# Holding each output unit behind the matmul emitted ahead of it, in the 512-token round of a two-stage mixture kernel

## The chip, the cores and the metric

The kernel runs on one core of a Trainium2 chip. A core has five engines that each work through a queue of their own in order: TensorE (PE: matmuls, with its weight loads as PEld), VectorE (DVE), ScalarE (ACT), GpSimd (POOL) and SyncE (SP, here only issuing DMAs). They wait for one another through semaphores. The metric is the device time of one execution in microseconds (us). Before the change it is 1851.79 us, the median of three runs (1851.22 to 1853.6).

## The reference

The result is three stages in a chain, all in float32.

```python
p_packed = sm_attn(p, k, v)                    # 32 packed queries per head, 576 keys
out = sm_attn(q, p_packed, p_packed)           # 4 batches x 8 heads x 576 tokens x 64
x = out.transpose(0, 2, 1, 3).reshape(2304, 512)
h = np.maximum(x @ w_in, 0.0)                  # 512 -> 2048
x = h * h @ w_out                              # 2048 -> 512
logits = x @ w_gate; P = np.exp(logits - logits.max())
for _ in range(8):                             # gate: rows, then columns
    P /= P.sum(1, keepdims=True) + 1e-09
    P /= P.sum(0, keepdims=True) + 1e-09
    P *= 2304 / 8
for e in range(8):                             # 8 experts, each over all 2304 tokens
    out += P[:, e:e+1] * (np.maximum(x @ w1[e], 0.0) @ w2[e])
```

## The kernel before

Every matmul operand is split into a high and a low part of a narrower format, and a product is three matmuls: high by high, high by low, low by high. The last stage, with the eight experts, takes most of the time. It treats the 2304 tokens in three rounds: 512 tokens (group p = 0, columns in blocks of 256), then 1024 (blocks of 512), then 768 (blocks of 384). This case is about the first of them, from about 414 to 757 us.

In that round `for n in range(NQ)` runs 32 units, a quarter of an expert's hidden width each. `unit(n, 0, ...)` computes the first layer by a Strassen-like scheme: seven products of 6 matmuls with 256 columns (`product`, L758), into three PSUM tiles X, Z and Y of 128x512:

- A11 into X; ACT copies X out (s1). A12 into Y; DVE adds s1 to Y.
- S1 into Z; ACT copies Z out (s5). S2 is added into X; ACT copies X out (s2).
- S4 is added into Z, after the copy s5 has read Z; DVE adds s2. S3 is added into X, after s2; DVE writes X + s5 into Y (L837). A22 is added into X, after that.

Four finished blocks are evacuated (`evac`): ACT writes the high part with the ReLU (L765, "hi" below), DVE the low part (L766, "lo"), and with that the second layer can start: `y_unit(n, t)` for t = 2, 3, 0, 1 multiplies the two hidden blocks of 128 rows by w2, 6 matmuls with 512 columns each (L788), into one of four PSUM tiles y0 to y3. These are the output units. They lag: `ys` begins with five empty entries, `unit` takes one entry at each of four places (`y()`), and the four of unit n are appended after it.

Three other streams share the queues. `split_w` makes the two parts of each weight block ahead of time: a load, for w1 four sums on DVE (`w1_sums`, L146 to L149), a copy on ACT (L177), a subtraction on POOL (L180). The gate's row and column sums are made in small steps (`hook`, `balance`): after unit 1 the maximum over all tokens (a DVE reduce, a matmul L704, a DVE reduce L705, a matmul L710), then from unit 2 to unit 7 sixteen half steps, in turn `rows_step` (five DVE operations, L718 to L723, the last of which writes `cs`) and `cols_step` (a matmul of 8 columns with `cs`, L728, then three DVE operations). These steps are emitted in `with pinned():`, which holds each instruction behind the last one emitted on its engine.

Nothing else fixes the order. The program is recorded in the order of the code; then a scheduler with a timing model of its own goes through it and puts on each engine the instruction that comes first in the code among those that its model finds ready. Where a product isn't ready in the model, a later output unit is drawn forward into the gap. `tc.issue_after(i)` adds an edge without a wait: what is recorded in the block stays behind instruction i on its engine.

Of the kernel before, what the change touches and what calls it, by code (L numbers as in the profile page):

```python
# [38 lines left out]
def kernel(ctx: ExitStack, tc: tile.TileContext, qT, kT, v, pT,  # L39
                                     win, wout, wg, w1, w2, out):  # L40
    nc = tc.nc
# [708 lines left out]
    def product(ps, n, p, a, b, start):  # L750

        i, o = WHERE[a]
        w, x = W["w1", n, i], XC[p, b]
        N = GROUPS[p][1]
        last = None
        for k in range(2):
            for u, v in ((0, 0), (0, 1), (1, 0)):
                last = nc.tensor.matmul(ps[:, :N], w[:, u, o + k * 128:o + (k + 1) * 128], x[v][:, k, :],  # L758
                                        start=(start and k + u + v == 0), stop=(k == 1 and u == 1), skip_group_check=True)
        return last  # L760

    def evac(key, src, p):
        N = GROUPS[p][1]
        h = hpa.tile([128, 2, N], F32R, tag="hh", name="hh", bufs=12)
        nc.scalar.activation(h[:, 0, :], src, AF.Relu)  # L765
        nc.vector.scalar_tensor_tensor(h[:, 1, :], src, 0.0, h[:, 0, :].bitcast(F32), op0=ALU.max, op1=ALU.subtract)  # L766
        H2[key] = h
# [34 lines left out]
    def small(N):  # L802
        return temps.tile([128, 512], F32, tag="s", name="s", bufs=4)[:, :N]

    def banks3():
        return [psm.tile([128, 512], F32, tag="c", name="psc", bufs=4) for _ in range(3)]

    def unit(n, p, ys, after):

        N = GROUPS[p][1]  # L810

        def y():
            if ys:
                ys.pop(0)()

        X, Z, Y = (t[:, :N] for t in banks3())
        s1 = small(N)
        product(X, n, p, "A11", "B11", True)
        nc.scalar.activation(s1, X, AF.Copy)
        at = product(Y, n, p, "A12", "B21", True)  # L820
        nc.vector.tensor_tensor(Y, Y, s1, op=ALU.add)
        evac((n, p, 0, 0), Y, p)
        y()
        after.get(0, lambda x: None)(at)
        s5 = small(N)
        product(Z, n, p, "S1", "T1", True)
        nc.scalar.activation(s5, Z, AF.Copy)
        s2 = small(N)
        at = product(X, n, p, "S2", "T2", False)
        nc.scalar.activation(s2, X, AF.Copy)  # L830
        after.get(1, lambda x: None)(at)
        y()
        product(Z, n, p, "S4", "B22", False)
        nc.vector.tensor_tensor(Z, Z, s2, op=ALU.add)
        evac((n, p, 0, 1), Z, p)
        at = product(X, n, p, "S3", "T3", False)
        nc.vector.tensor_tensor(Y, X, s5, op=ALU.add)  # L837
        evac((n, p, 1, 1), Y, p)
        after.get(2, lambda x: None)(at)
        y()  # L840
        at = product(X, n, p, "A22", "T4", False)
        evac((n, p, 1, 0), X, p)
        after.get(3, lambda x: None)(at)
        y()
# [87 lines left out]
    ys = [lambda: None] * 5  # L932
    for n in range(NQ):
        if n == EARLY + 1:
            ys.pop(0)()
        unit(n, 0, ys, {i: lambda at, n=n, i=i: hook(n, i, at) for i in range(4)})
        ys += y_units(n)
# [317 lines left out]
```

## Time and profile before

| | |
|---|---|
| median of three runs | 1851.79 us |
| profiled execution, its own time | 1851.22 us |
| its span | 1848.8 us |
| PE busy | 1829.9 us, 99% of the span |
| PEld / DVE / POOL / ACT busy | 90% / 69% / 58% / 45% |
| the chain that ended last | PE 95%, DVE 3%, ACT 1% |
| share of the chain by line | L758 37%, L1145 28% (psx 16%, psz 12%), L433 11%, L788 9% |

The span is the profiled execution from its first to its last instruction; 2.4 us of its time lie outside. The chain that ended last runs through TensorE nearly all the way, so a time in which TensorE waits is added to the whole, and work of another engine counts only where TensorE waits for it. TensorE's waits lie at the start, in the attention, and a few in the first third of the 512-token round.

### The profile page before, as it was taken

Reading aid. Unit: us, or ns where it says so; the run is one execution under the profiler, and the core shown is the slowest. Engines: PE = TensorE matmul, PEld = TensorE weight load, DVE = VectorE, ACT = ScalarE, POOL = GpSimd, SP = SyncE. Lnnn points to the kernel's source line nnn. Section 1 sums busy time; section 2 is a strip of 40 time slices with the busy share of each in tenths; the row PEclk is TensorE's granted clock in tenths of the full one; section 3 lists DMA queues with packets and bytes.
Section 4 is the critical chain, followed back from the end, with each engine's and each line's share of the span. In section 5 each row is a group of like instructions: output and inputs, shape, how many; then the busy total and the mean of one; then the engine's idle time right before and its main releaser. Section 6 shows DMA issues by size and latency. Waiting matters only on the chain.

```text
span 1848.8 us, 28664 instructions
## 1 busy us (share of the span) xinstructions
PE 1829.9 (99%) x10190; PEld 1661.8 (90%) x10190; DVE 1276.9 (69%) x2098; ACT 830.0 (45%) x1535; POOL 1074.2 (58%) x811
## 2 busy tenths in 40 slices
PE   8999999999999999999999999999999999999999
PEld 7899999998898898888888888888889999999998
DVE  5777777756666555687788877887775666666665
ACT  6767655545565555443333333333334323232233
POOL 4313322437699788287777877877764444444444
PEclk9999999999999999999999999999999999999999
DMA  7412211206799877677776777677788877778774
GB/s 279 160 35 69 79 37 46 103 21 236 256 319 334 294 268 275 215 226 269 238 240 237 222 268 249 226 249 230 245 311 265 277 255 262 261 253 262 260 251 148
DMA packets 166269, 403.55 MB, mean 218 GB/s; under 512 B 14208, under 2 KB 79984, under 8 KB 166128
## 3 DMA queue, kind: packets, MB, share of 16 engines
q1 hardware_dynamic: 131664, 346.15, 55.0%
q10 hardware_dynamic: 34464, 55.58, 9.8%
q8 instruction: 81, 1.33, 0.3%
q14 instruction: 60, 0.49, 0.1%
HBM read 273.96 MB, written 127.72 MB: 217 GB/s over the span
## 4 chain that ended last, share of the span: by engine, by line
PE 95%; DVE 3%; ACT 1%; issue 0%; DMA 0%; POOL 0%; SPq 0%; ACTq 0%; DVEq 0%; POOLq 0%
PE psc L758 37%; PE psx L1145 16%; PE psz L1145 12%; PE psy L433 11%; PE psy L788 9%; PE psh L414 5%; PE psh L367 1%; PE s L307 1%; PE pp L273 1%; PE s L245 0%; PE pslg L503 0%; DVE wt L146 0%; ACT w L177 0%; PE pso L1168 0%; DMA kt<-kT 0%
## 5 line engine op out<-in xcount | busy, mean ns | idle before, releaser
L758 PE MATMUL psc<-xc,w 128*128 128x256 f32 (+2 forms) x4032 | 777.4, 335 | 0.4 <-DVE hb L1051 0.4
L758 PEld LDWEIGHTS psc<-xc,w 128*128 128x128 f32 x4032 | 666.7, 188 | 65.4 <-DVE hb L1051 1.0
L1121 POOL TENSOR_TENSOR hh<-hb,hh 128x1024 fp32r<-128x1024 f32 (+1 forms) x224 | 504.6, 2256 | 372.2 <-ACT hh L1120 312.2
L1120 ACT ACTIVATE hh<-hb 128x1024 fp32r<-128x1024 f32 (+1 forms) x224 | 213.9, 955 | 448.3 <-DVE hb L1118 197.7
L1145 PE MATMUL psx<-hh,wa 128*128 128x512 f32 (+1 forms) x1536 | 352.7, 362 | 0.0
L1145 PEld LDWEIGHTS psx<-hh,wa 128*128 128x128 f32 x1536 | 278.9, 188 | 30.2 <-ACT hh L1120 0.4
L1145 PE MATMUL psz<-hh,wa 128*128 128x512 f32 (+1 forms) x1152 | 261.8, 362 | 0.3 <-issue 0.3
L1145 PEld LDWEIGHTS psz<-hh,wa 128*128 128x128 f32 x1152 | 209.0, 188 | 23.2 <-issue 0.9
L433 PE MATMUL psy<-h,w 128*128 128x320 f32 (+2 forms) x1200 | 224.7, 331 | 0.2
L180 POOL TENSOR_TENSOR w<-raw,w 128x256 fp32r<-128x256 f32 (+1 forms) x222 | 175.6, 823 | 64.9 <-ACT w L177 57.6
L788 PE MATMUL psy<-w,hh 128*128 128x512 f32 x768 | 200.8, 394 | 2.5 <-ACT hh L765 2.3
L1153 DVE TENSOR_TENSOR acc<-psx,acc 128x512 f32<-128x512 f32 (+1 forms) x248 | 151.9, 617 | 70.7 <-PE psx L1145 69.6
L433 PEld LDWEIGHTS psy<-h,w 128*128 128x128 f32 x1200 | 189.0, 188 | 12.3 <-ACT x L439 0.7
L1153 DVE TENSOR_TENSOR acc<-psz,acc 128x512 f32<-128x512 f32 (+1 forms) x184 | 112.5, 618 | 93.2 <-PE psz L1145 93.1
L1051 DVE SCALAR_TENSOR_TENSOR hb<-psc,gate 128x512 f32<-128x512 f32 (+1 forms) x256 | 157.1, 619 | 12.2 <-PE psc L758 7.3
L1025 POOL TENSOR_TENSOR wa<-rb,wa 128x512 fp32r<-128x512 f32 x80 | 132.6, 1666 | 49.7 <-DMA out<-acc 28.9
L788 PEld LDWEIGHTS psy<-w,hh 128*128 128x128 f32 x768 | 135.3, 189 | 25.0 <-ACT hh L765 3.1
L1118 DVE TENSOR_TENSOR hb<-hb 128x1024 f32<-128x1024 f32 (+1 forms) x96 | 133.4, 1390 | 28.9 <-POOL hh L1121 27.9
L414 PE MATMUL psh<-at,g 128*128 128x320 f32 (+2 forms) x768 | 123.7, 297 | 3.7 <-DVE g L377 2.4
L414 PEld LDWEIGHTS psh<-at,g 128*128 128x128 f32 x768 | 110.9, 189 | 8.3 <-issue 2.8
L180 POOL TENSOR_TENSOR w<-wt,w 128x256 fp32r<-128x256 f32 (+1 forms) x124 | 91.5, 767 | 31.8 <-issue 21.9
L129 POOL TENSOR_TENSOR ca<-ca,cc 128x512 int32<-128x512 int32 x28 | 36.7, 1312 | 99.0 <-ACT cc L128 90.4
(157 smaller groups left out, 1838.9 us busy)
## 6 DMA issues: line engine op xcount, KB each, us to landing
w<-kept_w SPq DMA_DIRECT2D x184, 512.0 KB, 4.6
kept_w<-wa SPq DMA_DIRECT2D x112, 512.0 KB, 4.7
wa<-kept_w SPq DMA_DIRECT2D x112, 512.0 KB, 4.7
kept_w<-w SPq DMA_DIRECT2D x96, 512.0 KB, 4.5
raw<-w ACTq DMA_DIRECT2D x58, 512.0 KB, 5.1
rb<-w ACTq DMA_DIRECT2D x64, 256.0 KB, 4.3
w<-kept_w SPq DMA_DIRECT2D x61, 256.0 KB, 4.3
raw<-win SPq DMA_DIRECT2D x16, 512.0 KB, 3.8
```

The costliest lines, as they stand in the source:

```text
L180: nc.gpsimd.tensor_tensor(w[:, 1, o:o + step], t[:, o:o + step], w[:, 0, o:o + step].bitcast(F32), op=ALU.subtract)
L414: nc.tensor.matmul(ps[:, u - begin:w - begin], gw[:, x, m * 128:(m + 1) * 128], at[:, y, g, u - b * S:w - b * S], start=(i == 0), stop=(i ...
L433: nc.tensor.matmul(ps[:, :n], w[:, x, d * 128:(d + 1) * 128], h[:, y, :], start=(i == 0), stop=(i == 11))
L758: last = nc.tensor.matmul(ps[:, :N], w[:, u, o + k * 128:o + (k + 1) * 128], x[v][:, k, :], start=(start and k + u + v == 0), stop=(k == 1 ...
L788: nc.tensor.matmul(ps, h[:, x, o:o + 128], w[:, y, :], start=(n % 4 + m + x + y == 0), stop=(n % 4 == 3 and m == 1 and x == 1), skip_group ...
L1025: nc.gpsimd.tensor_tensor(w[:, 1], src, w[:, 0].bitcast(F32), op=ALU.subtract)
L1051: nc.vector.scalar_tensor_tensor(HB[q][m, t][:, nn, :], src, 0.0, GATE[p, g // 4][:, t * N:(t + 1) * N], op0=ALU.max, op1=ALU.mult)
L1118: nc.vector.tensor_tensor(src, src, hb[MINUS[k]], op=ALU.subtract)
L1120: nc.scalar.activation(hi, src, AF.Copy)
L1121: nc.gpsimd.tensor_tensor(lo, src, hi.bitcast(F32), op=ALU.subtract)
L1145: nc.tensor.matmul(ps, A2[q, k][:, u, nn, d * 128:(d + 1) * 128], OPS[7 * q + k][v][:, nn, :], start=(first and nn + u + v == 0), stop=(nn ...
L1153: nc.vector.tensor_tensor(a, ps, a, op=ALU.add)
```

## The change

A helper is added that finds the last instruction recorded on TensorE so far, and each output unit is recorded behind it. The products keep their freedom, and so do the DVE and ACT instructions of an output unit.

```diff
+    def last_pe():
+        return tc.issue_after(next(i for i in reversed(nc.cur_bb.bb.instructions) if i.engine == mybir.EngineType.PE))
+
     def unit(n, p, ys, after):
...
         def y():
             if ys:
-                ys.pop(0)()
+                with last_pe():
+                    ys.pop(0)()
```

The last TensorE instruction recorded ahead of a `y()` is the product just before it, or, where a hook has recorded a gate matmul in between, that matmul. The `y()` of units 0 to 31 are concerned; one output unit at the start of unit 11 and the four that are left for the next round are taken elsewhere, without the edge. TensorE's order differs from the first output unit to the first products of the next round, and is the same, matmul for matmul, before and after that stretch. Line numbers behind the diff grow by four.

The names below: psc_4814, psc_4815 and psc_4816 are X, Z and Y of unit 1, psc_4944 to psc_4946 those of unit 2. The operand xc0_4181 holds B11 and B21, xc0_4364 T1 and T2, xc0_4182 B22 and T3, xc0_4365 T4, so that S1 is the row that writes Z from 4364, S4 the one that writes Z from 4182, S3 writes X from 4182 and A22 writes X from 4365.

TensorE in unit 1, from S1 to S3, before:

```order
L758 MATMUL psc_4815<-xc0_4364,w_4389 128x256 x6
L788 MATMUL psy_4862<-w_4776,hh_4755 128x512 x2
L788 MATMUL psy_4916<-w_4776,hh_4755 128x512 x2
L788 MATMUL psy_4937<-w_4776,hh_4786 128x512 x3
L788 MATMUL psy_4965<-w_4776,hh_4786 128x512 x3
L788 MATMUL psy_4937<-w_4853,hh_4832 128x512
L788 MATMUL psy_4965<-w_4853,hh_4832 128x512
L758 MATMUL psc_4815<-xc0_4182,w_4525 128x256 x6
L758 MATMUL psc_4814<-xc0_4182,w_4525 128x256 x6
```

The same place now, from unit 0's A22 on:

```order
L758 MATMUL psc_4678<-xc0_4365,w_4372 128x256 x6
L788 MATMUL psy_4862<-w_4772,hh_4745 128x512
L758 MATMUL psc_4816<-xc0_4181,w_4379 128x256 x6
L788 MATMUL psy_4862<-w_4772,hh_4745 128x512
L788 MATMUL psy_4862<-w_4776,hh_4755 128x512
L758 MATMUL psc_4815<-xc0_4364,w_4389 128x256 x6
L788 MATMUL psy_4862<-w_4776,hh_4755 128x512 x2
L758 MATMUL psc_4815<-xc0_4182,w_4525 128x256 x6
L758 MATMUL psc_4814<-xc0_4182,w_4525 128x256 x6
L758 MATMUL psc_4814<-xc0_4365,w_4530 128x256 x6
```

Between S1 and S4 stood twelve output matmuls and now stand two; between S3 and A22 stood eight and now none.

ACT in that place now, from the evacuation of unit 0's A22 to unit 1's copies s5 (s_4837) and s2 (s_4845):

```order
L765 ACTIVATE hh_4786<-psc_4678 128x256
L177 ACTIVATE w_4791<-raw_4535 128x512
L177 ACTIVATE w_4797<-wt_4703 128x512
L177 ACTIVATE w_4803<-wt_4703 128x512
L177 ACTIVATE w_4809<-raw_4535 128x256
L177 ACTIVATE w_4853<-raw_4674 128x512
L177 ACTIVATE w_4857<-raw_4674 128x512
L111 DMA raw_4789<-w2 128x1024
L177 ACTIVATE w_4891<-raw_4676 128x512
L765 ACTIVATE hh_4832<-psc_4816 128x256
L831 ACTIVATE s_4837<-psc_4815 128x256
L834 ACTIVATE s_4845<-psc_4814 128x256
```

Seven weight copies stand ahead of s5; before, there were the same seven and one more, between hh_4832 and s5.

TensorE in unit 2 before, first from S1 to S4 and then from S3 to the column step:

```order
L758 MATMUL psc_4945<-xc0_4364,w_4797 128x256 x6
L788 MATMUL psy_4937<-w_4974,hh_4962 128x512
L788 MATMUL psy_4965<-w_4974,hh_4962 128x512
L788 MATMUL psy_4937<-w_4974,hh_4962 128x512 x2
L788 MATMUL psy_4965<-w_4974,hh_4962 128x512 x2
L758 MATMUL psc_4945<-xc0_4182,w_4803 128x256 x6
...
L788 MATMUL psy_4937<-w_4978,hh_5073 128x512 x2
L788 MATMUL psy_4965<-w_4978,hh_5073 128x512 x2
L788 MATMUL psy_4937<-w_4978,hh_5073 128x512
L788 MATMUL psy_4965<-w_4978,hh_5073 128x512
L728 MATMUL psy_5081<-cs_5059,ones_94 128x8
```

In the part left out stand S3, four output matmuls, A22 and eight more. The same place now, from the matmul of the maximum on:

```order
L710 MATMUL psy_4983<-grow_4911,ones_94 128x1
L758 MATMUL psc_4945<-xc0_4364,w_4797 128x256 x6
L758 MATMUL psc_4945<-xc0_4182,w_4803 128x256 x6
L758 MATMUL psc_4944<-xc0_4182,w_4803 128x256 x6
L788 MATMUL psy_4916<-w_4853,hh_4876 128x512 x3
L788 MATMUL psy_4916<-w_4857,hh_4886 128x512 x3
L758 MATMUL psc_4944<-xc0_4365,w_4809 128x256 x6
L728 MATMUL psy_5081<-cs_5059,ones_94 128x8
L788 MATMUL psy_4937<-w_4853,hh_4832 128x512 x3
L788 MATMUL psy_4937<-w_4857,hh_4929 128x512 x3
```

S4 now follows S1 directly (six output matmuls before), and six output matmuls and A22 stand between S3 and the column step (eighteen and A22 before). Units 4 and 6 read the same in both points; there six output matmuls of before between S1 and S4 are gone too.

DVE at the second reduce of the maximum (L705), before:

```order
L705 TENSOR_REDUCE grow_4911<-psy_4913 1x1
L821 TENSOR_TENSOR psc_4946<-psc_4946,s_4947 128x256
L766 SCALAR_TENSOR_TENSOR hh_4962<-psc_4946,hh_4962 128x256
L146 TENSOR_TENSOR wt_5004<-raw_4835 128x256
L148 TENSOR_TENSOR wt_5004<-raw_4835 128x256
```

And now:

```order
L825 TENSOR_TENSOR psc_4946<-psc_4946,s_4947 128x256
L766 SCALAR_TENSOR_TENSOR hh_4962<-psc_4946,hh_4962 128x256
L146 TENSOR_TENSOR wt_5004<-raw_4835 128x256
L148 TENSOR_TENSOR wt_5004<-raw_4835 128x256
L705 TENSOR_REDUCE grow_4911<-psy_4913 1x1
```

The reduce moved behind four operations of unit 2. From unit 11 on the pattern is steady: between a unit's S1 and its S4 stand three or four output matmuls and the next unit's A11, where before there were seven to sixteen and that A11.

## Rows read from the trace of the kernel before

**Rows 1.** Windows by stage: busy us of each engine (count), granted clock, DMA.

```profile
414.00:460.00 46.00, 44.64 (x287) 39.86 (x287) 28.12 (x69) 24.51 (x62) 30.80 (x44) 1.00 0.67 234
460.00:506.00 46.00, 44.86 (x281) 40.12 (x280) 31.83 (x91) 24.01 (x57) 31.92 (x46) 1.00 0.77 256
506.00:552.00 46.00, 46.00 (x292) 41.60 (x291) 28.62 (x57) 28.16 (x66) 41.39 (x53) 1.00 0.90 317
```

**Rows 2.** Chain of waits, 425 to 450 us: start, length, what.

```profile
427.85 2.74 PE psy L788 x12
430.58 1.43 PE psc L758 x12
```

**Rows 3.** Waits of TensorE, 400 to 760 us: total, times, longest.

```profile
PE psy L788 <- ACT hh L765: 2.3, 5, 0.7
```

**Rows 4.** Timeline of TensorE: start, length, what, idle before it.

```profile
444.88 1.20 PE L788 MATMUL psy<-w,hh 128*128 128x512 f32 x4 [0.68 <-ACT hh L765]
...
449.82 0.28 PE L728 MATMUL psy<-cs,ones 128*128 128x8 f32 x2
```

**Rows 5.** Timeline of ACT, units 1 and 2.

```profile
424.16 0.39 ACT L765 ACTIVATE hh<-psc 128x256 fp32r<-128x256 f32 x1 [1.34 <-PE psc L758]
...
428.13 0.63 ACT L177 ACTIVATE w<-wt 128x512 fp32r<-128x512 f32 x1
428.66 0.38 ACT L827 ACTIVATE s<-psc 128x256 f32<-128x256 f32 x1
...
441.42 0.38 ACT L827 ACTIVATE s<-psc 128x256 f32<-128x256 f32 x1 [0.20 <-PE psc L758]
...
444.46 0.36 ACT L765 ACTIVATE hh<-psc 128x256 fp32r<-128x256 f32 x1
```

**Rows 6.** Timeline of DVE: X + s5, a lo, the row step's end.

```profile
444.24 0.43 DVE L837 TENSOR_TENSOR psc<-psc,s 128x256 f32<-128x256 f32 x1 [0.21 <-PE psc L758]
...
445.65 0.42 DVE L766 SCALAR_TENSOR_TENSOR hh<-psc,hh 128x256 fp32r<-128x256 f32 x1 [0.37 <-ACT hh L765]
...
447.81 0.43 DVE L723 TENSOR_REDUCE cs<-P 128x8 f32<-128x144 f32 x1
...
467.62 0.43 DVE L837 TENSOR_TENSOR psc<-psc,s 128x256 f32<-128x256 f32 x1 [0.21 <-PE psc L758]
...
470.90 0.43 DVE L723 TENSOR_REDUCE cs<-P 128x8 f32<-128x144 f32 x1
...
490.28 0.43 DVE L837 TENSOR_TENSOR psc<-psc,s 128x256 f32<-128x256 f32 x1 [0.21 <-PE psc L758]
...
493.59 0.44 DVE L723 TENSOR_REDUCE cs<-P 128x8 f32<-128x144 f32 x1
```

**Rows 7.** Timeline of DVE, around the reduce L705 and unit 2's weight sums.

```profile
422.59 1.00 DVE L146 TENSOR_TENSOR wt<-raw 128x256 f32<-128x256 f32 x1
...
437.27 0.28 DVE L705 TENSOR_REDUCE grow<-psy 1x1 f32<-1x128 f32 x1 [1.82 <-POOL grow L702]
438.44 0.43 DVE L821 TENSOR_TENSOR psc<-psc,s 128x256 f32<-128x256 f32 x1 [0.89 <-PE psc L758]
439.32 0.42 DVE L766 SCALAR_TENSOR_TENSOR hh<-psc,hh 128x256 fp32r<-128x256 f32 x1 [0.45 <-ACT hh L765]
439.66 2.73 DVE L146 TENSOR_TENSOR wt<-raw 128x256 f32<-128x256 f32 x1
```

**Rows 8.** Timeline of POOL in that place.

```profile
437.19 4.93 POOL L180 TENSOR_TENSOR w<-raw,w 128x256 fp32r<-128x256 f32 x7
```

**Rows 9.** All of line L146: minimum, median, maximum in ns.

```profile
L146 DVE TENSOR_TENSOR wt<-raw x30: 403/426/2733, 419.8 to 726.8; 128x256 f32<-128x256 f32 x30
```

**Rows 10.** Windows in the attention stage, with the granted clock.

```profile
34.00:38.00 4.00, 0.98 (x8) 0.53 (x6) 3.70 (x9) 3.03 (x9) 1.92 (x2) 1.00 0.45 140
38.00:44.00 6.00, 5.79 (x30) 5.48 (x31) 3.76 (x7) 4.70 (x8) 2.93 (x4) 0.72 0.29 90
48.00:52.00 4.00, 1.63 (x8) 1.08 (x7) 3.91 (x11) 3.52 (x7) 2.41 (x3) 1.00 0.96 340
```

## The prediction

> **What bounds the kernel now.** I read the windows by stage first. From 506 us on TensorE is busy without a break in the 512-token round, while DVE, ACT and POOL are not; in the two windows before, it is busy for 44.64 and 44.86 of 46 us [rows 1]. So the round is bound by TensorE, and what can be won in the stretch that this change reorders is about the 2.5 us of these two windows. Second, TensorE's list of waits: nearly all of that, 2.3 us, is one kind, five times an output unit that waits for ACT's evacuation of the unit's S4 block [rows 3]; the timeline shows one of them, 0.68 us at 444.88 [rows 4]. These are output units that were drawn forward so far that their input was not there. Third, the chain of waits gives the price of a matmul when nothing waits: 2.74/12 = 0.228 us with 512 columns, 1.43/12 = 0.119 us with 256 [rows 2], so a product of six is 0.715 us. No price depends on what stands beside it, so an order without waits costs the same as any other. The question is which waits go and which come.
>
> **What the change removes.** In the new order an output unit follows S4 of its own unit by 2.8 us of TensorE work or more (1.4 in unit 0), where in the five places that waited it followed by 0.71 to 0.76. All five waits go: -2.3 us.
>
> **What it adds.** The output matmuls that were drawn forward were filling gaps, and some of these gaps are real. I count for each dependence how much TensorE work stands in it now, and compare it with how long the other engine takes. A turn through ACT after a product: ACT starts 0.20 us after TensorE's last matmul and copies for 0.38 us [rows 5]; the evacuation that ended the wait at 444.88 was done at 444.46 + 0.36 = 444.82, so TensorE starts 0.06 us after ACT. That is 0.64 us.
>
> 1. S1 to S4 in units 2, 4 and 6. Nothing stands between them now, and S4 must wait for the copy s5: 0.64 us each, 1.92 in sum (1.6 if a turn takes little more than 0.5; 3.5 if a weight copy of 0.53 us, item 2, stands ahead of each). In the odd units S2 and six output matmuls (2.1 us) stand there, which covers it.
>
> 2. S1 to S4 in unit 1. Here ACT is late as well: seven weight copies stand ahead of s5. In the trace the evacuation of unit 0's A22 starts at 424.16 and s5 at 428.66, with these seven and one more between; the eighth takes 428.66 - 428.13 = 0.53 [rows 5]. Now s5 starts 0.20 + 4.50 - 0.53 = 4.17 us after A22's end and lets S4 go at 4.17 + 0.38 + 0.06 = 4.61. TensorE's work in that time is two products and five output matmuls, 1.43 + 1.14 = 2.57. It waits 2.04 us. Before, twelve output matmuls stood in the gap and hid all of it. Faster copies than one per 0.53 us are not in the trace, so at least 1.7; a copy that waits for its block adds up to one copy, 2.6.
>
> 3. S3 to A22 in unit 1, with nothing between: DVE starts 0.21 us after S3, takes 0.43 [rows 6], and 0.06 to start again: 0.70 us (0.5 to 1.1 with another DVE operation in the way).
>
> 4. The matmul L710 in unit 2 needs the reduce L705, which moved behind two weight sums. From A12's end: 0.21 to the sum on Y, 1.30 from there to the end of lo (438.44 to 439.74), two sums, the reduce 0.28 [rows 7]. TensorE comes there after twelve output matmuls and S2, 3.46 us. With 1.00 us for a sum beside a busy POOL (422.59) the chain is 0.21 + 1.30 + 2.00 + 0.28 + 0.06 = 3.85, and TensorE waits 0.4 us. But this very sum took 2.73 us at 439.66, up to the end of a run of seven POOL subtractions of 0.70 us [rows 7, 8]; then it is 2.1, and 3.7 if the sum stands through all of the run. Its median over 30 is 0.43 and 2.73 is the maximum [rows 9], so I take 0.4 and keep 0 and 3.7. [...]
>
> 5. The column step L728 in units 2, 4 and 6. This is the largest term. `cs` comes from a DVE chain that starts at S3's end: X + s5, two lo, five row operations with a third lo among them. From L837 to the end of L723 it takes 448.24 - 444.24 = 4.00, 471.33 - 467.62 = 3.71 and 494.03 - 490.28 = 3.75 us [rows 6]; with 0.21 ahead and 0.06 behind, 4.27, 3.98 and 4.02 from S3's end. Before, eighteen output matmuls and A22 (4.8 us) stood in it, and L728 at 449.82 came 1.6 us after `cs` [rows 4, 6]. Now only six and A22 stand there, 6 x 0.228 + 0.715 = 2.08, since the next output unit is recorded behind L728 and held there. The next unit's products stand behind L728 in both orders. DVE's order in the chain hardly changes. So TensorE waits 2.19 + 1.90 + 1.94 = 6.03 us. Two of the chain's operations can wait for ACT; one did at 445.65, for 0.37 us [rows 6]. Without both it is 0.7 us shorter each time, 3.9 in sum; with one more weight copy of 0.53 us in ACT's way each time, 7.6. All that TensorE has left is queued behind the waiting matmul, so these waits are full price.
>
> The other column steps, in the units between, have 5.6 us and more of work in the chain and stay free. Sum: 1.92 + 2.04 + 0.70 + 0.4 + 6.03 = 11.1 of new waits, less 2.3, is +8.8 us. TensorE is the bound to the end, so nothing gives it back. Made against the profiled execution, whose own time is 1851.22: **1860.0 us**. (That execution is the fastest of the three; against the median it is +8.2 us or 0.44%.) The lower ends together give 1.6 + 1.7 + 0.5 + 0 + 3.9 = 7.7, +5.4, 1856.6; the upper ones 3.5 + 2.6 + 1.1 + 3.7 + 7.6 = 18.5, +16.2, 1867.4.
>
> **Rivals.**
>
> *The row sums are there in time* (not slower). Place: the three L728; price: 6.0 us; it decides when `cs` is done within 2.1 us of S3's end. Then 1860.0 - 6.0 = 1854.0, which is +0.12% on the median, no change that can be told. For it: the waits of items 1 and 4 just ahead give ACT and DVE time to work off what stands in their queues. Against it: three samples between 3.98 and 4.27, and 0.7 us less is not enough. 12%.
>
> *No new wait at all*, because the gaps of the order are covered by something that I don't see: 1851.22 - 2.3 = 1848.9, -0.16%. The new order stands fixed with L728 ahead of the held units, and the five waits in [rows 3] show that TensorE doesn't pass a waiting matmul by. 4%.
>
> *The clock falls in the gaps.* [...] 9%. [...]
>
> *ACT is late in the steady part.* From unit 11 on about 1.63 us of work stand between S1 and S4, where 2.3 to 4.4 stood. The turn needs 0.64; it fails only if ACT still has 1 us to do when S1 ends, two weight copies. With 0.3 us in each of 22 units: +6.6, 1866.6. Against it: ACT is busy for 28 of 46 us there [rows 1]. Weight blocks are freed later too, since the output units that read them run later; each is written again by one ACT copy of 0.53 and two POOL subtractions of 0.70 us, and by my count of TensorE work at least 8 us still lie between its last reader and the first of its next content (12 before). 9%.
>
> **How the numbers follow.** The forecast has 66%. "Same" is within 0.2% (3.7 us) of the median, about what three runs can tell from no change. Slower: 66 + 9 + 9, less 2 for a forecast that misses low, is 82%; same 12 + 2 and part of the 4, 15%; faster 3%. The range for 8 in 10 runs from 1854.5, which leaves out most of the two cases without the L728 waits, to 1867.
>
> **What would show it.** The waits of TensorE after: the five on L765 gone; three on L728 for DVE's L723 of about 2 us each; L758 for ACT's s5 four times, 2.0 us once and 0.6 three times; L758 for DVE's X + s5 once; L710 for DVE's L705 up to 0.4. Windows 414 to 506 us lose some 9 us of TensorE's busy share, those after it none. It is wrong if L728 doesn't wait, if the windows after 506 show idle time, or if the granted clock falls below 1.00 there.

## The result, and the profile after

The changed kernel takes 1866.97 us, the median of four runs (1864.93 to 1868.04), against 1852.69 for the kernel before beside it (1851.22 to 1855.37): a ratio of 1.0076 (95% interval 1.0064 to 1.0089), 14 us slower. Forecast was slower, by 8.8 us. The profiled execution is the slowest of the four (1868.04 us, span 1865.9), and that of before the fastest of its four (1851.22, span 1848.8), so the two traces lie 17.1 us apart and the medians 14.3.

The windows that answer to [rows 1], one later stretch, and seven microseconds by themselves (busy us of PE, PEld, DVE, ACT, POOL with counts; then the granted clock, the DMA share and GB/s):

```profile
414.00:460.00 46.00, 38.90 (x237) 33.88 (x236) 26.99 (x58) 21.30 (x54) 27.87 (x40) 0.93 0.61 219
460.00:506.00 46.00, 41.87 (x261) 37.14 (x261) 31.83 (x88) 24.11 (x54) 29.62 (x41) 1.00 0.67 231
506.00:552.00 46.00, 46.00 (x288) 41.34 (x287) 28.55 (x57) 26.89 (x63) 37.53 (x48) 1.00 0.74 259
552.00:644.00 92.00, 89.18 (x555) 79.34 (x554) 64.51 (x110) 49.73 (x114) 80.44 (x97) 1.00 0.90 320
442.00:449.00 7.00, 5.95 (x23) 5.46 (x24) 2.47 (x7) 3.06 (x8) 1.58 (x3) 0.51 0.60 212
```

Up to 506 us TensorE now stands still for 7.10 + 4.13 us, where it stood still for 1.36 + 1.14. Two things were not in the sum: a granted clock of 0.51 from 442 to 449 us (by half microseconds 0.50 from 442.5 to 448.5, and 1.00 up to 442 and from 449 on), and 2.82 us of idle time between 552 and 644, where before there was none.

TensorE's list of waits, 400 to 780 us, that answers to [rows 3] (total, times, longest):

```profile
PE psy L728 <- DVE cs L723: 4.4, 3, 1.6
PE psc L758 <- ACT s L831: 3.6, 6, 1.6
PE psy L710 <- DVE grow L705: 3.1, 1, 3.1
PE psc L758 <- ACT s L823: 2.6, 3, 1.4
PE psc L758 <- DVE psc L841: 0.5, 1, 0.5
```

The five waits on L765 are gone, and of the new ones four lines of five are those forecast. The fourth, products that wait for the copy s1 (L823), was not. The places, in TensorE's timeline (start, length, what, the idle time before it and what ended it):

```profile
428.06 1.70 PE L758 MATMUL psc<-xc,w 128*128 128x256 f32 x12 [1.58 <-ACT s L831]
430.28 0.98 PE L758 MATMUL psc<-xc,w 128*128 128x256 f32 x6 [0.53 <-DVE psc L841]
...
442.58 0.58 PE L710 MATMUL psy<-grow,ones 128*128 128x1 f32 x2 [3.12 <-DVE grow L705]
443.02 1.63 PE L758 MATMUL psc<-xc,w 128*128 128x256 f32 x6
...
449.76 0.87 PE L758 MATMUL psc<-xc,w 128*128 128x256 f32 x6
451.88 0.39 PE L728 MATMUL psy<-cs,ones 128*128 128x8 f32 x2 [1.25 <-DVE cs L723]
452.12 1.63 PE L788 MATMUL psy<-w,hh 128*128 128x512 f32 x6
453.59 1.59 PE L758 MATMUL psc<-xc,w 128*128 128x256 f32 x12
...
476.25 0.39 PE L728 MATMUL psy<-cs,ones 128*128 128x8 f32 x2 [1.59 <-DVE cs L723]
...
567.58 1.70 PE L758 MATMUL psc<-xc,w 128*128 128x256 f32 x12 [1.35 <-ACT s L823]
```

Two readings. The six matmuls at 443.02, right behind the wait on L710, take 1.63 us where six take 0.87 to 0.98 elsewhere: the granted clock there, from 443 to 445 us, is 0.50. And a wait costs more than its figure: A22 at 449.76 is 0.715 us of work, from one start to the next where nothing waits, but shown as 0.87, since the end of a run is modelled and lies 0.16 behind the point where the next run could have started. And the first run behind a wait is 0.11 longer (1.70 for 1.59, 0.98 for 0.87). So I put each wait at about 0.27 more than it shows, an estimate from these two differences. At L728, from 449.76 to 453.59, it is 3.83 us for 0.715 + 0.15 (L728) + 1.39 = 2.25 of work: the wait shown as 1.25 costs 1.58, 0.33 more.

Why L710 waited, in DVE's and POOL's timelines (answering to [rows 7, 8]):

```profile
437.29 4.70 DVE L146 TENSOR_TENSOR wt<-raw 128x256 f32<-128x256 f32 x1
441.92 0.41 DVE L148 TENSOR_TENSOR wt<-raw 128x256 f32<-128x256 f32 x1
442.25 0.27 DVE L705 TENSOR_REDUCE grow<-psy 1x1 f32<-1x128 f32 x1
```

```profile
436.84 4.87 POOL L180 TENSOR_TENSOR w<-raw,w 128x256 fp32r<-128x256 f32 x7
```

One weight sum, 0.43 us by its median in [rows 9], lasted until 0.28 us after POOL's seven subtractions were through, and the reduce that the maximum waits for stood behind it. The late wait at 567 us has the same root. DVE, POOL and ACT ahead of it:

```profile
562.91 2.06 DVE L148 TENSOR_TENSOR wt<-raw 128x256 f32<-128x256 f32 x1
564.89 0.96 DVE L147 TENSOR_TENSOR wt<-wt,raw 128x256 f32<-128x256 f32 x1
```

```profile
562.66 2.03 POOL L449 TENSOR_TENSOR xc<-x,xc 128x768 fp32r<-128x768 f32 x1
```

```profile
565.88 0.63 ACT L177 ACTIVATE w<-wt 128x512 fp32r<-128x512 f32 x1 [3.42 <-DVE wt L147]
566.42 0.83 ACT L448 ACTIVATE xc<-x 128x768 fp32r<-128x768 f32 x1
567.16 0.36 ACT L823 ACTIVATE s<-psc 128x256 f32<-128x256 f32 x1
```

The sum L148 ends 0.28 us after POOL's L449; ACT's copy of the sums waits for the next one, and s1 stands behind that copy and another in ACT's queue. The waits at 590 and 612 us have the same sum of 2.06 us ahead of them.

### The profile page after: what moved, and what is told of

Its sections match the earlier page's. It is cut to its first block, busy times and chain, and to the rows that moved or that the text cites. A ratio compares the mean times of both kernels' runs of the same rounds, so it can differ in the third digit from the quotient of the medians.

```text
span 1865.9 us, 28662 instructions
## 1 busy us (share of the span) xinstructions
PE 1836.4 (98%) x10190; PEld 1664.7 (89%) x10190; DVE 1303.8 (70%) x2098; ACT 834.6 (45%) x1535; POOL 1079.4 (58%) x811
## 3 DMA queue, kind: packets, MB, share of 16 engines
q1 hardware_dynamic: 131664, 346.15, 54.5%
## 4 chain that ended last, share of the span: by engine, by line
PE 61%; DVE 1%; issue 0%; DMA 0%; ACT 0%; ACTq 0%; DVEq 0%
PE psc L758 30%; PE psx L1149 16%; PE psz L1149 12%; PE psy L788 2%; PE pso L1172 0%; DVE rb L1026 0%; DVE hb L1055 0%; DMA out<-wo 0%; DVE rb L1025 0%; ACT wo L1177 0%; DVE psc L1092 0%; DVE psc L1075 0%; DVE rb L1024 0%; DVE psc L1097 0%; ACT s L831 0%
```

## The experiments

Times are medians. Ratios are to the kernel before on the same chip, with 95% intervals, and a difference with a plus sign is worked out from the ratio; the changed kernel stands at 1.0076 from the first measurement and 1.0091 from the second (e5). The traces are of one execution each.

**e1, e2: the early part and the late part apart.**

```diff
-                with last_pe():
+                with last_pe() if n < 8 else ExitStack():    # e1; n >= 8 in e2
```

> Only the output units of units 0 to 7 are held. By the waits of the trace after the change, those behind 552 us (1.35 + 0.25 + 0.61 + 0.61 + 0.32 = 3.1 us, products that wait for ACT's copies s1 and s5) belong to the part from unit 8 on, and the rest to the first eight units: then this kernel is 14.3 - 3.1 = 11.2 us over the kernel before (about 1863.9), with the waits up to 510 us unchanged and none behind. Rival: the late waits are an after-effect of the early ones (weight blocks that come late), then they stay and so does the time, +14.3.

1863.68 us, 1.0062 (1.0049 to 1.0075): +11.5 us (12.1 between the medians), as expected. The early waits are the same to 0.1 us, and behind 506 us there is none.

> Only the output units from unit 8 on are held. If the steady pattern itself brings the late waits, +3.1 us for them and about -0.9 for two of the five old waits (units 6 and 7, whose output units are now held): +2.2 us over the kernel before. Rival: the steady pattern is free and the late waits came from the early part: then -0.9, not to be told from before.

1858.19 us, 1.0034 (1.0021 to 1.0047): +6.3 us. The late waits are there in full (1.34, 0.25, 0.61 and 0.61 us from 558 to 603), with the early part as before: the held pattern makes them by itself. The size was missed, since where the two orders meet (units 6 to 8) too few output units were left to fill gaps: 0.53, 0.48, 0.62, 0.41 and 0.62 us between 490 and 514.

**e3: the reduce ahead of the sums.**

```diff
-        nc.vector.tensor_reduce(row[0:1, :], ps[0:1, :], axis=AX.X, op=ALU.max, negate=True)
+        nc.vector.tensor_reduce(row[0:1, :], ps[0:1, :], axis=AX.X, op=ALU.max, negate=True); steps["reduce"] = nc.cur_bb.bb.instructions[-1]
...
-                    sums_ahead(n + 2)
+                    with tc.issue_after(steps["reduce"]): sums_ahead(n + 2)
```

> All held as in the change, and the weight sums of unit 2's hook are held behind the reduce L705, so that DVE does the reduce before the two sums; TensorE's and ACT's order is the same, row for row. Theory: TensorE's wait of 3.12 us on L710 comes from the one sum that lasted 4.70 us beside a run of seven POOL subtractions, and the clock of 0.52 and 0.63 behind it (about 3 us) comes from that gap. Then the wait on L710 goes and the granted clock stays at 1.00; the sum still lasts as long as POOL's run, now ahead of L838 and L841 on DVE, so A22 and the column step of unit 2 are held up instead (A22 by about 0.6, L728 by 2 to 3 us): in all about 4 us less than the change, +10 us over before (range +8 to +12). Rival: the reduce was late for another reason, or the clock falls whatever stands on L710: then the time stays within 1 us of the change's, and the clock falls in the same place.

1866.16 us, 1.0075 (1.0062 to 1.0088): of the 4 us hoped for, almost nothing in the median, and outside the expected +8 to +12. The trace shows the mechanism as expected and the clock not (DVE, then TensorE, then a window):

```profile
437.04 0.27 DVE L705 TENSOR_REDUCE grow<-psy 1x1 f32<-1x128 f32 x1
437.24 4.54 DVE L146 TENSOR_TENSOR wt<-raw 128x256 f32<-128x256 f32 x1
```

```profile
446.92 0.39 PE L728 MATMUL psy<-cs,ones 128*128 128x8 f32 x2 [2.30 <-DVE cs L723]
```

```profile
448.00:452.00 4.00, 4.00 (x18) 3.72 (x17) 0.23 (x2) 0.60 (x2) 0.00 (x0) 0.57 0.37 139
```

The wait on L710 is gone; the sum still lasts as long as POOL's run, holds up L838 and L841, and L728 waits 2.30 us. Behind that wait the clock falls, instead of behind the other.

**e4: an output unit ahead of the column step.**

```diff
-        after.get(3, lambda x: None)(at)
-        y()
+        if n in (2, 4, 6):
+            y()
+            after.get(3, lambda x: None)(at)
+        else:
+            after.get(3, lambda x: None)(at)
+            y()
```

> All held as in the change, but in units 2, 4 and 6 the fourth output unit is recorded ahead of the column step instead of behind it; nothing else moves on TensorE. Theory: the chain to cs starts at S3's end whatever TensorE does next, so six output matmuls (1.39 us) in the gap take 1.39 us off each of the waits of 1.25, 1.59 and 1.59 us: 1.25 + 1.39 + 1.39 = 4.0 us less than the change, +10.3 over before. Rival: the time is set by what follows the column step (DVE's P, the next half step), so that the output unit taken from behind L728 is missing there and the gain is given back: then within 1 us of the change.

1865.6 us, 1.0069 (1.0055 to 1.0082): 14.0 us over the median of before, so by its time the edit gained nothing that can be told, where 4.0 us were expected. The waits on L728 are what the theory says, 0, 0.22 and 0.22 instead of 1.25, 1.59 and 1.59 us. But 1.0 us came back as longer waits for s5 at 702 and 745 us (0.57 and 0.71, where the change has 0.32 in all). At the latter place the trace of the change shows ACT not busy: ahead of 746.39 it stands idle for 2.23 us until DVE's L825, which comes after four sums of 0.42 to 1.00 us beside a POOL run of 5.47 us. In the traces the round is 2.6 us shorter than the change's; the median doesn't show it.

**e5: the changed kernel once more.**

> The changed kernel itself, on the same chip as the next three. About 14.3 us over the kernel before, with the same waits; a second trace of it tells how much of its time differs from execution to execution (the other traces so far reach the 512-token round up to 2 us apart, and the clock falls at other places).

1868.11 us, 1.0091 (1.0077 to 1.0104). Its trace differs from the first in one stretch (TensorE, a window, then DVE):

```profile
428.74 2.75 PE L758 MATMUL psc<-xc,w 128*128 128x256 f32 x12 [1.58 <-ACT s L831]
```

```profile
429.00:435.00 6.00, 5.47 (x22) 4.89 (x22) 2.24 (x6) 2.46 (x6) 6.00 (x10) 0.50 1.02 326
```

```profile
440.74 0.51 DVE L146 TENSOR_TENSOR wt<-raw 128x256 f32<-128x256 f32 x1
441.17 0.97 DVE L148 TENSOR_TENSOR wt<-raw 128x256 f32<-128x256 f32 x1
442.06 0.27 DVE L705 TENSOR_REDUCE grow<-psy 1x1 f32<-1x128 f32 x1
```

The clock fell behind unit 1's wait, not unit 2's. TensorE came to unit 2 later, but so did the sum: in both traces the output matmuls ahead of L710 end 2.17 us after the sum's start (439.46 and 437.29, 442.91 and 440.74). The sum took 0.51 us instead of 4.70, and L710 did not wait at all. So the wait of 3.1 us on L710 is not in every execution of this order; the traces of e1, e4 and e8 have it too.

**e6: the four sums on POOL.**

```diff
-        s1, s2, s3, s4 = (t[:, j * 256:(j + 1) * 256] for j in range(4))
+        s1, s2, s3, s4 = (t[:, j * 256:(j + 1) * 256] for j in range(4)); eng = nc.gpsimd if n == 4 else nc.vector
-        nc.vector.tensor_tensor(s1, a21, a22, op=ALU.add)
+        eng.tensor_tensor(s1, a21, a22, op=ALU.add)
...
```

> The change, with the four weight sums of unit 4's block (those that stood ahead of L705) on POOL instead of DVE. TensorE's order is the same, row for row. Theory: it is the sum shut out for the length of POOL's run that holds up first L705, then (where the reduce went ahead) L838 and L841; with no sum on DVE there the wait of 3.12 us on L710 goes, L728 of unit 2 waits 1.25 us as before or less, and with the long gap goes the fall of the clock behind it (3 us): 6 us less than the change, +8 over before. Rival: the clock falls from the waits of unit 1 and 2 together, whichever is left; then only 3 us less, and the granted clock still shows 0.5 between 440 and 455 us.

1863.5 us, 1.0067 (1.0054 to 1.0080), 4.6 us less than the change on the same chip. No wait on L710, 1.37 us on L728 in unit 2, and the clock is 1.00 all the way from 426 to 506 us. The direction is the theory's, three quarters of the size.

**e7: useless matmuls in the gap.**

```diff
-        ps = ybank()[:, 0:1]
-        nc.tensor.matmul(ps, ones, steps["row"], start=True, stop=True)
+        ps = ybank(); [nc.tensor.matmul(ps[:, 256:512], W["w1", 2, 0][:, 0, 0:128], XC[0, "B21"][0][:, 0, :], start=True, stop=True) for _ in range(20)]
+        nc.tensor.matmul(ps[:, 0:1], ones, steps["row"], start=True, stop=True); ps = ps[:, 0:1]
```

> The change, with 20 useless products of 256 columns (2.4 us) on TensorE ahead of the matmul L710, in the gap; they write an unused part of its PSUM tile. Theory: the clock fell because TensorE stood still. Then L710 waits 1.4 us instead of 3.1, half of an output unit moves behind it and covers the wait of 0.47 on s5, the granted clock stays at 1.00 up to 506 us, and the time is 2.5 to 3 us shorter than the change's although more is computed. Rival: the fall has another cause (load of the chip, matmuls of this stretch): then it stays, and the time is that of the change within 0.5 us.

1870.31 us, 1.0101 (1.0086 to 1.0117): 2.2 us above the change beside it, which the intervals don't tell apart. As a test of the price it failed: in its profiled execution the sum took 0.57 us, so there was no gap to fill. POOL's run of seven beside it was longer than the 4.87 us in the first trace of the change:

```profile
438.39 5.65 POOL L180 TENSOR_TENSOR w<-raw,w 128x256 fp32r<-128x256 f32 x7
```

What the run shows is where the clock fell, behind a wait of 1.69 us on L728 and once more far behind, after DVE's L146 had waited 2.38 us, up to 720.24, for a weight load:

```profile
450.00:455.00 5.00, 5.00 (x22) 4.46 (x22) 1.11 (x4) 0.93 (x3) 0.00 (x0) 0.66 0.40 153
...
728.00:731.00 3.00, 3.00 (x14) 2.96 (x15) 0.70 (x2) 1.43 (x4) 3.00 (x4) 0.56 0.26 105
```

```profile
727.77 2.93 PE L758 MATMUL psc<-xc,w 128*128 128x256 f32 x12 [2.52 <-ACT s L831]
```

**e8: the operands' low parts on DVE.**

```diff
-        operand(1, name, t, nc.vector if i % 2 else nc.gpsimd)
+        operand(1, name, t, nc.vector)
```

> The change, with all low parts of the operands of the next round (L449) on DVE; four of the seven were on POOL, 2.03 us each. Theory of the late waits: the weight sum L148 is shut out for the whole of POOL's L449 (2.06 beside 2.03 us at 562.7), ACT's copy of the sums waits for it, and s1 stands behind that copy. Then the waits of 1.35, 0.61 and 0.61 us on s1 at 567, 590 and 612 us go: 2.6 us less than the change, +11.7 over before. Rival: ACT itself is behind in the steady part; then the waits stay, or move to s5, and the time stays within 1 us of the change.

1866.21 us, 1.0080 (1.0066 to 1.0094), 1.9 us less than the change beside it, with intervals that overlap. In the trace the waits of 1.35, 0.61 and 0.61 us on s1 are 0, 0.22 and 0; one on s5 grew from 0.25 to 1.00. So in the trace the late waits hang on POOL's L449, and a part of them moves rather than goes: 3.1 us in five waits became 1.5 us in three.

**e9: three of these edits together** (e4, e6 and e8).

> The change with three of the edits so far put together: the fourth output unit of units 2, 4 and 6 ahead of the column step, the weight sums beside L705 on POOL, and the operands' low parts on DVE. If the waits of the traces are the whole of the loss and add up, there is left: 1.57 + 0.53 in unit 1, three times 0.47 on s5, about 0.5 on L728, and 1.2 to 2.2 in the steady part, 5.2 to 6.2 us, with 0.1 for each restart about 1 more, less the 2.3 + 0.5 of the kernel before: +3.5 to +4.5 us over before if the clock stays at 1.00, and up to 3 us more where it falls behind the wait of unit 1. Rival: something that no wait shows costs time in the held order (the chain of weights, more work on TensorE); then it stays near the change's, +10 or more.

1857.75 us, 1.0033 (1.0021 to 1.0045): +6.1 us. TensorE's list of waits, 400 to 780 us:

```profile
PE psc L758 <- ACT s L831: 5.0, 7, 1.6
PE psc L758 <- DVE psc L841: 0.5, 1, 0.5
PE psy L728 <- DVE cs L723: 0.4, 2, 0.2
PE psc L758 <- ACT s L823: 0.2, 1, 0.2
```

Eleven waits, 6.2 us, where before had five with 2.3; with 0.27 for each of six more that is 5.5, and the two spans lie 5.9 apart (1854.7 and 1848.8). The clock stayed at 1.00 from 426 to 506. So nothing large is hidden from the list of waits. The time lies above the +3.5 to +4.5 expected, since I had put the cost of a restart too low (0.1 us, where the differences above give 0.27). By the medians the three edits took 0.3, 4.6 and 1.9 us singly, and together they take 8 to 11 us, depending on which measurement of the change they are set against; the trace of e9 is also one without a fall of the clock.

**e10, e11, e12: a version from the kernel before.** In units 2 to 7 one output unit is held, and behind S3 of its own unit.

```diff
-        at = product(X, n, p, "S3", "T3", False)
+        at = product(X, n, p, "S3", "T3", False); steps["S3", n] = nc.cur_bb.bb.instructions[-1]
...
+    def held(unit, i):
+        with tc.issue_after(i):
+            unit()
...
         ys += y_units(n)
+        if 2 <= n < 8:
+            ys[-1] = lambda last=ys[-1], n=n: held(last, steps["S3", n])
```

> The kernel before, with one output unit of units 2 to 7 held: the one for tokens 128 to 255 (t = 1) behind the S3 product of its own unit, so that three of the six output matmuls between S1 and S4 stand between S3 and the output unit that needs S4's evacuation. By the trace of before its turn takes 1.40 us from S4's end, and S3 (0.72) and three output matmuls (0.69) make 1.41; between S1 and S4 0.69 are left for a turn of 0.64. Then the five waits on L765 (2.3 us in sum) go and none comes: -2.3 us with five restarts of 0.1, -2.5 to -2.8 us, 0.14 per cent. Rival: 0.69 between S1 and S4 is too little (ACT has other work), or the wait moves to A22 (X + s5); then no change, within 1 us.

1851.82 us, 1.0002 (0.9993 to 1.0010): no change. Of the five waits one is left, of 0.60 us, and a product waits 0.54 for X + s5; but far behind, at 537.36, a product waits 2.26 us for s1. (The profiled execution is the slowest of eleven, and 1.8 us of its lag lie ahead of the round.) TensorE, DVE and POOL there:

```profile
537.36 0.98 PE L758 MATMUL psc<-xc,w 128*128 128x256 f32 x6 [2.26 <-ACT s L819]
```

```profile
529.55 5.36 DVE L146 TENSOR_TENSOR wt<-raw 128x256 f32<-128x256 f32 x1
```

```profile
527.61 7.02 POOL L180 TENSOR_TENSOR w<-raw,w 128x256 fp32r<-128x256 f32 x10
```

The same thing again, a sum that lasts to the end of POOL's run. Behind this wait the matmuls keep their pace: the product at 538.88 takes 0.71 us from start to start. e11 adds the edit of e8:

> The last kernel (one output unit of units 2 to 7 behind S3, from the kernel before) with the operands' low parts on DVE as well, so that POOL's run of ten subtractions, beside which the sum L146 lasted 5.36 us at 529.6, follows another pattern. If that sum was what took the gain back (2.26 us of waiting for s1 at 537), the wait goes and the gain of the early part shows: 1.2 to 1.7 us less than before, about 1850. Rival: DVE has 1.2 us more to do four times and another sum meets a run: then a wait of 1 to 2 us at another place, and no change within 1 us.

1849.19 us, 0.9987 (0.9978 to 0.9996): 2.3 us faster than the kernel before, and the fastest of all. That is more than the 1.2 to 1.7 us expected; the interval excludes a ratio of 1, and the gain in it is 0.7 to 4.1 us. The wait at 537 is gone, the sum at that place takes 0.44, and these are all waits from 400 to 780 us:

```profile
PE psy L788 <- ACT hh L765: 0.7, 1, 0.7
PE psc L758 <- DVE psc L837: 0.6, 1, 0.6
```

> The control to the last one: the kernel before with the operands' low parts on DVE and nothing held. The kernel before has no wait of TensorE in the steady part, so there is nothing to win there: no change within 1 us, and the five waits on L765 stay (2.3 us in sum). Rival: the gain of the last kernel came from the operands alone; then about 2 us less than before here too.

1851.56 us, 0.9999 (0.9990 to 1.0008), with the five waits as before: the gain is not from the operands alone, nor by e10 from the held units alone.

## Why the prediction came out as it did

The direction, the places and the mechanism were right: TensorE is the bound, the waits that the change removes are worth little, and the drawn-forward output units were filling real gaps. The prices held in the new order: six output matmuls take 1.39 us from start to start and a product 0.71, as medians over the round, in both traces. The time came out at 1866.97, 7 us above the forecast and just inside the upper edge of the range at 1867. That it lies inside is luck: the second measurement (e5) has 1868.11. By one of its own signs the forecast was wrong, since a window after 506 us shows idle time (2.82 us between 552 and 644). The granted clock stayed at 1.00 there, but fell to 0.51 from 442 to 449 us, which the sum had left out. Term by term, as waits shown (us), in the two traces of the changed kernel:

| term | forecast | trace 1 | trace 2 (e5) |
|---|---|---|---|
| five waits on L765 removed | -2.3 | -2.3 | -2.3 |
| 1. S1 to S4, units 2, 4, 6 | 1.92 | 1.41 | 1.41 |
| 2. S1 to S4, unit 1 | 2.04 | 1.58 | 1.58 |
| 3. S3 to A22, unit 1 | 0.70 | 0.53 | 0.53 |
| 4. L710 for L705 | 0.4 | 3.12 | 0 |
| 5. L728, units 2, 4, 6 | 6.03 | 4.43 | 4.78 |
| sum | +8.8 | +8.8 | +6.0 |
| late waits (s1, s5) | 0 | 3.1 | 3.1 |
| halved clock | 0 | 2.9 | 2.7 |
| 0.27 for each wait more (9 and 8) | 0 | 2.4 | 2.2 |

The column of trace 1 ends at 17.2, and the spans lie 17.1 apart, 0.2 of it ahead of the round. That of trace 2 ends at 14.0; its span is 14.8 us longer, of which 0.9 lie ahead of the round. That the sum comes to 8.8 in trace 1 is chance: item 4 was 2.7 too low, the others together 2.7 too high. The halved clock is priced from its windows: 5.95 us busy at 0.51 in 442 to 449, so 5.95 x 0.49 = 2.9, and 5.47 x 0.50 = 2.7.

- **Items 1, 2, 3 and 5** show 0.17 to 0.59 less per wait than I worked out (trace 2). In good part that is how a wait is shown: with the 0.27 added, 0.47 becomes 0.74 (forecast 0.64) and 1.59 becomes 1.86 (forecast 1.90 and 1.94). I left the 0.27 out on both sides, and it counts for the nine waits more. L728 of unit 2 is smaller in trace 1 (1.25): of the work ahead of it the six output matmuls took 1.91 us from start to start instead of 1.39, partly at the granted clock of 0.50 (up to 448.5 us), and filled more of the gap.
- **Item 4 is the term that was mis-sized.** Of its two ends (0 and 3.7) I took the median's side, because 2.73 us was one sample in thirty. Trace 1 shows a sum of 4.70 us beside a POOL run of 4.87, near the upper end; e3 shows it again (4.54), and e10 in another place (5.36 in a run of 7.02). In e5, with the same order, it takes 0.51. Both ends were real, and which one comes differs between executions; what decides it stays open, since in e7 the sum started 0.46 us into POOL's run and took 0.57, and in trace 1 it started at 0.45 and took 4.70. In e7 the four sums took 0.57 to 0.96 us each, and POOL's seven subtractions beside them 5.65 us instead of 4.87. In trace 1, e3 and e10 the sum lasts as long as 6.5 to 7.7 subtractions of 0.70 us and ends 0.28 us after the last of the run; what holds it there was not shown.
- **The clock** I gave 9%. In the first trace of the change and in those of e1, e3, e4, e5, e7 and e8 it fell to 0.50 to 0.66 in the window behind a wait, in e2, e6, e9 and e10 not. It fell behind each of the four waits of 3.1 us on L710, behind 2.30 (e3) and 2.52 (e7), but not behind 2.26 (e10, by the pace of the matmuls), and behind those of 1.2 to 1.7 us only twice (e5, e7), while most of these kept 1.00. One fall costs 2.7 to 2.9 us, an estimate from the windows of e5 and trace 1. The stretch of [rows 10] that kept 1.00, from 48 to 52 us, doesn't speak against a fall: in trace 1 TensorE is busy there for the same 1.63 us, and the granted clock from 52 to 57 us is 0.66. That standing still brings the fall about is what the places suggest, since each lies behind a wait. It was not shown by filling a gap, since e7 had none to fill.
- **ACT late in the steady part** I also gave 9%, at 0.3 us in each of 22 units. It came, with 3.1 us in five places, and e2 shows it by itself. But the place was mostly s1, not s5, and there ACT was late because DVE's sums were, beside POOL; in the trace of e8 1.6 us of it are gone. My evidence against it, ACT's busy share, looked at the wrong engine: between 552 and 644 us DVE's busy time rose from 54.5 to 64.5 us, with 110 operations where there had been 115.

So the waits that were forecast came where they were forecast. What the forecast had too small or at nothing is what stands behind them: the weight sums held up beside POOL (0.4 us for the early part, nothing for the late one), the fall of the clock and the cost of each restart.

## What to carry to other kernels

An order in which work fills gaps is not improved by pinning it to the order of the code; look for each wait that goes at what stood in the gaps of the others, and hold only the one piece that came too early (e11, which also moves the operands' low parts, holds six output units of 128 and gains, where the change holds nearly all and loses). Count a wait of TensorE at what it shows plus the restart (about 0.27 us here), and add the stretch at a granted clock of 0.50 that may stand behind it (2.7 to 2.9 us here). And where a DVE sum like L146 stands beside a run of POOL subtractions, look at the case that it lasts to the end of the run (4.70 us here), and not only at its median (0.43), when something on the critical path is queued behind it.

## What the runs showed of the hardware

- The DVE sum L146, 0.43 us by its median in the kernel before, lasted 2.73 us (before), 4.70 (the change), 4.54 (e3) and 5.36 (e10) beside a run of POOL subtractions, each time to about 0.3 us after the run's end; in other executions (e5, e7) the four sums beside such a run took 0.51 to 0.97 us each.
- The same program differs from execution to execution in where TensorE's clock falls: to 0.50 from 429 to 435 us, behind a wait of 1.58 us in unit 1 (e5), or to 0.51 from 442 to 449 us, at a wait of 3.12 us in unit 2 (trace 1). Behind a wait of 2.26 us (e10) a product took the usual 0.71 us.
- By my estimate a wait of TensorE costs about 0.27 us more than the idle time shown in this profile: 0.16 between the point where the next run could have started and the modelled end of the last (0.87 for 0.715), 0.11 in the longer run behind (1.70 for 1.59). With it the waits of e9 make 5.5 us of the 5.9 between its span and that of before.
